# A gated mix of windowed attention and a small routed MLP on one core: another written order for all five engines, projections interleaved by halves, and 112 small operations on other engines

## The chip, the cores and the metric

The kernel runs on one core of a Trainium2 chip, in one launch. The metric is device time in microseconds (us). A profile of one execution shows TensorE as PE (matmuls) and PEld (weight loads), VectorE as DVE, ScalarE as ACT, GpSimd as POOL and the sync engine, which issues most DMAs, as SP. Each engine runs its own list of instructions in order and waits at semaphores for the others.

## The reference

All tensors are bf16. `x` has 2048 rows of 512.

```python
g = sigmoid((x * gate_w).sum(-1, keepdims=True))
# A: attention, 32 heads of 16, each query sees the 256 keys up to itself
qkv = x @ wqkv;  scores = q @ k.T / 4;  p = softmax(masked scores);  a = (p @ v) @ wo
# B: the 8 rows with the largest r = x @ w_r pass through an MLP, the others unchanged
idx = argsort(-r)[:8]
y = (silu(x[idx] @ w_gate) * (x[idx] @ w_up)) @ w_down * sigmoid(r[idx])
b = x;  b[idx] += y
out = g * a + (1 - g) * b
```

In the call both branches get the same `x` (`A_x`).

## The kernel before

The 512 features are cut into four chunks `c` of 128 (eight heads each), the 2048 rows into four column tiles `tc` of 512. For each (`c`, `tc`) there are three **projections**, Q, K and V, into one bank of PSUM (`psG`, two banks). Those of the first column tile of chunk 0 run on the full array (L607, four matmuls over 128 rows). All others are cut by the contraction into 64-row matmuls (L614): four on one half of the array's rows, then four on the other, eight matmuls of 512 columns into the same bank. Matmuls on different halves can run side by side. Their results are taken up by small operations: Q is cast to `QT` (L582/L584), K is cast to `Kr` (L570) and multiplied by four head masks into the block-diagonal `Kbd` (L573, four operations), V is transposed by 32-blocks into `VT` (L589) and multiplied by two masks into `Vbd` (L593, two operations).

The **attention** goes in 156 score units. A main unit takes two blocks of 32 keys against 256 queries: four matmuls (L644), two on each half. A tail unit takes the last 32 queries of eight blocks: 16 matmuls of 32 columns. Each unit writes one of two buffers in `psS`; one ACT instruction (L655) takes the exponential of it into `PT`, and the unit after next has to wait for that. The triangle of each block is masked on `PT` (L665: 128x128 for a main unit, 128x512 for a tail unit). Probabilities times values are `psO` matmuls (L684), pairs of 34 columns on both halves, called pv below. DVE normalises them and applies the gate (L711, L723, L727), a transposing DMA brings them to `OT` (L757), and the output projection (L778, eight matmuls of 64 rows, like a projection) is added to `(1-g)*b` on DVE (L783) and stored.

The **router** needs the two products of `x` with `w_r` and `gate_w` (L804, 64 matmuls of 2 columns), a search of the eight largest on DVE (MAX8, FIND_INDEX8: L828, L829), a gather on the POOL queue, then the MLP on eight rows (L858: 112 matmuls of 8 columns; L900: 14 of 512 columns).

**What sets the order.** The program is recorded as a list of nodes with their dependences. A table `ORDER` holds for every engine the numbers of its nodes in the order in which they are emitted (negative numbers are the bulk loads, held back by `GATE` until a numbered unit's exponential). `BANK` gives each `psG` user its bank and the half it starts with. `FILL` puts filler matmuls (L534) ahead of some units. Waits follow from the dependences and the order. So nothing is decided at run time but how long an engine waits. Before, `BANK` mixes both starting halves.

## Time and profile before

| | us |
|---|---|
| median of 3 runs | 184.43 (184.06 to 184.55) |
| the profiled execution: its own time | 183.18 |
| its span, first to last instruction | 181.1 |
| PE / ACT / DVE / POOL busy | 168.3 / 137.1 / 119.0 / 70.1 |
| first exponential starts | 8.56 |
| last exponential ends | 170.16 |

Busy time is the union of an engine's instructions. A 512-column matmul is shown for about 0.38 us, though the next on the same half starts 0.22 us later, so a PE that is shown busy isn't full. The granted clock of TensorE was 0.977 of full speed on the mean. In the timeline a row gives the start, the length, the engine, the operation and how many were merged into the row; in brackets stands the idle time before it and what ended it. In a table by stage each engine has its busy time and, in brackets, its number of instructions.

### The profile page before, as it was taken

Reading aid. Unit: us, or ns where it says so; the run is one execution under the profiler, and the core shown is the slowest. Engines: PE = TensorE matmul, PEld = TensorE weight load, DVE = VectorE, ACT = ScalarE, POOL = GpSimd, SP = SyncE. Lnnn points to the kernel's source line nnn. Section 1 sums busy time; section 2 is a strip of 40 time slices with the busy share of each in tenths; the row PEclk is TensorE's granted clock in tenths of the full one; section 3 lists DMA queues with packets and bytes.
Section 4 is the critical chain, followed back from the end, with each engine's and each line's share of the span. In section 5 each row is a group of like instructions: output and inputs, shape, how many; then the busy total and the mean of one; then the engine's idle time right before and its main releaser. Section 6 shows DMA issues by size and latency. Waiting matters only on the chain.

```text
span 181.1 us, 10051 instructions
## 1 busy us (share of the span) xinstructions
PE 168.3 (93%) x4586; PEld 119.6 (66%) x4587; DVE 119.0 (66%) x311; ACT 137.1 (76%) x165; POOL 70.1 (39%) x153
## 2 busy tenths in 40 slices
PE   6989999999999999999999999999999999999870
PEld 2446764878686668866878466768876777776520
DVE  7959677988958482351966578776738462726690
ACT  1387721899988898676899698879998999988310
POOL 1054160426339844320554434543441525442200
PEclk9999999999999999957999999999999999999998
DMA  6992162633176754225494121621022551145321
GB/s 138 207 214 81 38 196 54 143 93 105 62 172 162 131 145 141 62 63 153 125 195 92 29 62 34 125 60 29 13 81 79 72 151 38 31 121 177 118 92 42
DMA packets 35745, 18.68 MB, mean 103 GB/s; under 512 B 27617, under 2 KB 35569, under 8 KB 35569
## 3 DMA queue, kind: packets, MB, share of 16 engines
q1 hardware_dynamic: 34560, 17.71, 41.0%
q8 instruction: 37, 0.61, 1.5%
q10 hardware_dynamic: 1072, 0.26, 0.7%
q14 instruction: 12, 0.09, 0.2%
q0 software_dynamic: 64, 0.02, 0.0%
HBM read 11.81 MB, written 4.20 MB: 88 GB/s over the span
## 4 chain that ended last, share of the span: by engine, by line
PE 69%; DVE 12%; ACT 7%; issue 6%; DMA 2%; SPq 1%; POOL 0%; POOLq 0%; DVEq 0%
PE f_psO L684 23%; PE f_psG L614 19%; PE f_psS L644 17%; ACT f_PT L655 7%; PE f_psG L778 4%; DVE f_Kbd L573 2%; DMA out_dram<-f_outt 2%; DVE f_PT L512 2%; PE f_psG L900 2%; PE f_psG L858 2%; DVE f_QT L584 1%; DVE f_VT L589 1%; DVE f_On L727 1%; PE f_psG L804 1%; DVE f_outt L783 1%
## 5 line engine op out<-in xcount | busy, mean ns | idle before, releaser
L655 ACT ACTIVATE f_PT<-f_psS 128x1024 bf16<-128x1024 f32 (+2 forms) x156 | 133.7, 917 | 25.5 <-PE f_psS L644 23.7
L684 PE MATMUL f_psO<-f_Vbd,f_PT 64*128 64x34 bf16 x2880 | 88.0, 175 | 0.7 <-DVE f_On L727 0.7
L684 PEld LDWEIGHTS f_psO<-f_Vbd,f_PT 64*128 64x128 bf16 x2880 | 73.9, 93 | 17.3 <-DVE f_On L727 2.8
L614 PE MATMUL f_psG<-f_XT,f_W 64*128 64x512 bf16 x360 | 83.9, 382 | 0.8 <-DVE f_QT L584 0.5
L644 PE MATMUL f_psS<-f_QT,f_Kbd 64*128 64x256 bf16 (+2 forms) x960 | 71.5, 225 | 1.8 <-ACT f_PT L655 0.6
L665 POOL TENSOR_TENSOR f_PT<-f_PT,f_MK 128x128 bf16<-128x128 bf16 x96 | 41.0, 437 | 81.1 <-ACT f_PT L655 77.9
L644 PEld LDWEIGHTS f_psS<-f_QT,f_Kbd 64*128 64x128 bf16 x960 | 36.6, 93 | 14.1 <-ACT f_PT L655 5.7
L614 PEld LDWEIGHTS f_psG<-f_XT,f_W 64*128 64x128 bf16 x360 | 25.2, 94 | 9.3 <-PE f_psG L614 1.3
L593 POOL TENSOR_SCALAR f_Vbd<-f_VT,f_pb 128x512 bf16<-128x512 f32 x32 | 24.0, 752 | 17.3 <-DVE f_wrg L792 9.2
L778 PE MATMUL f_psG<-f_wo,f_OT 64*128 64x512 bf16 x112 | 27.6, 375 | 0.5 <-DVE f_outt L783 0.4
L665 DVE TENSOR_TENSOR f_PT<-f_PT,f_MK 128x128 bf16<-128x128 bf16 (+1 forms) x60 | 18.4, 326 | 10.7 <-ACT f_PT L655 10.6
L573 DVE TENSOR_SCALAR f_Kbd<-f_Kr,f_hm 128x512 bf16<-128x512 bf16 (+2 forms) x68 | 24.9, 406 | 0.4 <-PE f_psS L644 0.3
L570 DVE CAST f_Kr<-f_psG 128x512 bf16<-128x512 f32 (+2 forms) x17 | 11.4, 668 | 11.9 <-PE f_psG L614 11.4
L783 DVE SCALAR_TENSOR_TENSOR f_outt<-f_xr,f_omg_f,f_psG 128x512 bf16<-128x512 bf16 x15 | 11.1, 743 | 8.6 <-issue 5.3
L584 DVE CAST f_QT<-f_psG 128x512 bf16<-128x512 f32 (+1 forms) x16 | 10.6, 660 | 6.4 <-PE f_psG L614 6.0
L589 DVE STREAM_TRANSPOSE f_VT<-f_psG 128x512 f32<-128x512 f32 x16 | 11.4, 711 | 3.6 <-PE f_psG L614 3.5
L711 DVE RECIPROCAL f_RC<-f_psO 128x32 f32<-128x32 f32 (+1 forms) x17 | 5.9, 344 | 11.9 <-PE f_psO L684 11.7
L727 DVE TENSOR_TENSOR f_On<-f_psO,f_RG 128x512 bf16<-128x512 f32 (+1 forms) x17 | 11.2, 658 | 0.5
L778 PEld LDWEIGHTS f_psG<-f_wo,f_OT 64*128 64x128 bf16 x112 | 7.9, 93 | 2.4 <-issue 0.6
L523 PE MATMUL f_psS<-f_RC 128*128 128x512 bf16 x10 | 4.2, 606 | 1.7 <-DVE f_qi L453 1.7
L723 DVE TENSOR_TENSOR f_RG<-f_RC,f_g_f 128x32 f32<-128x32 f32 (+1 forms) x17 | 3.9, 228 | 0.5
L582 ACT ACT_TABLE_LOAD x1 | 1.3, 1283 | 3.7 <-DVE f_MK L508 3.7
(103 smaller groups left out, 63.5 us busy)
## 6 DMA issues: line engine op xcount, KB each, us to landing
f_xc<-in_A_x_dram SPq DMA_DIRECT2D x8, 256.0 KB, 3.6
f_xr<-f_xc SPq DMA_DIRECT2D x16, 128.0 KB, 3.0
out_dram<-f_outt SPq DMA_DIRECT2D x16, 128.0 KB, 2.1
f_big<-in_B_w_up_dram SPq DMA_DIRECT2D x8, 224.0 KB, 2.9
f_big<-in_B_w_gate_dram SPq DMA_DIRECT2D x8, 224.0 KB, 3.9
f_OT<-in_B_w_down_dram SPq DMA_DIRECT2D x4, 256.0 KB, 3.3
f_W<-in_A_wqkv_dram SPq DMA_DIRECT2D x2, 384.0 KB, 3.9
f_wo<-in_A_wo_dram SPq DMA_DIRECT2D x4, 128.0 KB, 3.0
```

Of the source, the lines that this page charges most:

```text
L573: add("dve", lambda e, h=h: e.tensor_scalar(out=Kbd[:, sl, a // 32:(a + n) // 32, h, :], in0=Kr[:, kr, a:a + n].rearrange("p (a k) -> p a ...
L584: add("dve", lambda e: e.tensor_copy(out=dst, in_=psG[:, it.r, 0:n]), item=it, w=ks, occ=70 + 1.04 * n, due=due, cls="ev")
L589: add("dve", lambda e: e.transpose(out=VT[:], in_=psG[:, it.r, :]), item=it, w=[("VT", vb)], occ=630, due=due, cls="ev")
L593: add(VENG, lambda e, o=o, i=i, b=b: e.tensor_scalar(out=o, in0=i, scalar1=pb_[:, b:b + 1], scalar2=1.0, op0=ALU.mult, op1=ALU.mult), r=[( ...
L614: return e.matmul(psG[:, it.r, 0:n], W[P, kc, which, 128 * c:128 * c + 128], XT[P, kc, 512 * tc + a:512 * tc + a + n], start=(k8 == 0), st ...
L644: ins[s] = e.matmul(psS[:, sb2 + s, n * k:n * k + n], Kbd[P, kslot[(c, kb // 16)][0], kb % 16].rearrange("p h k -> p (h k)"), QT[P, c % 2, ...
L655: add("act", lambda e: e.activation(out=oa, in_=ia, func=ACT.Exp, scale=0.25), r=[("S", i % 2)], w=pk_ + [("ex", i)], occ=2 * nk * n * 0.8 ...
L665: add(eng, lambda e: e.tensor_tensor(out=v, in0=v, in1=m, op=ALU.mult), r=MKR + pk_, w=pk_, occ=cost, due=at(i + 1), cls="mk")
L684: ins[r] = e.matmul(psO[:, r, 68 * ji + 34 * s:68 * ji + 34 * s + 34], PT[P, s, o0:o0 + 128], Vbd[P, c % 2, s, kb, :], start=(kb == kbs[0] ...
L727: add("dve", lambda e: e.tensor_tensor(out=o, in0=i0_, in1=i1_, op=ALU.mult), r=["O", "RG"], w=[("On", ob, 0), ("On", ob, 1)], occ=60 + 12 ...
L778: return e.matmul(psG[:, it.r, :], OTrun(c, a, 1)[P], wo[P, c, :], start=(k8 == 0), stop=(k8 == 7), tile_position=(64 * x, 0), skip_group_ ...
L783: add("dve", lambda e: e.scalar_tensor_tensor(out=outt[:, xs, :], in0=xr[:, xs, :], scalar=omg_f[:, a:a + 1], in1=psG[:, it.r, :], op0=ALU ...
```

## The change

Every list of `ORDER` is written anew, with `GATE`, `FILL` and `BANK`. The recorded nodes are the same but for the filler matmuls: 27 before, 8 now. In `BANK` all split projections now start with the same half, and the second half of one projection stands in the list among the first half of the next one, which has the other bank. 112 operations stand in another engine's list: 72 go from POOL to DVE, 37 from DVE to POOL and three from DVE to ACT. The net effect: of the 68 `Kbd` operations 11 are now on POOL; of the 32 `Vbd` operations 15 are on DVE; of the 128 small masks 75 are on DVE (32 before); of the 28 tail masks 12 are on POOL (none before); three `Kr` casts are on ACT.

The code gets an alternative engine for these nodes, and the planner's costs of them are written out:

```diff
+        for e in self.ENGS:
+            for op in queue[e]:
+                assert op.eng == e or op.alt[0] == e
+                op.eng = e
...
+        def cast(e, o, i):
+            return e.copy(out=o, in_=i) if e is nc.scalar else e.tensor_copy(out=o, in_=i)
...
-            add("dve", lambda e: e.tensor_copy(out=Kr[:, kr, a:a + n], in_=psG[:, it.r, 0:n]), item=it,
-                w=[("Kr", kr, b) for b in ks], occ=70 + 1.04 * n, due=due, cls="ev")
+            add("dve", lambda e: cast(e, Kr[:, kr, a:a + n], psG[:, it.r, 0:n]), item=it,
+                w=[("Kr", kr, b) for b in ks], occ=70 + 1.04 * n, due=due, cls="ev", alt=("act", 55 + 0.83 * n))
...
-                    r=[("Kr", kr, b) for b in ks] + [("hm", h)], w=[("Kbd", sl, h, b) for b in ks], occ=40 + 0.5 * n, due=due + 1, cls="kb")
+                    r=[("Kr", kr, b) for b in ks] + [("hm", h)], w=[("Kbd", sl, h, b) for b in ks], occ=40 + 0.5 * n, due=due + 1, cls="kb", alt=("pool", 100 + 2.86 * n))
...
-                    r=[("VT", vb), ("pb", b)], w=[("Vbd", c % 2, tc, b)], occ=780, due=due + 2, cls="vb")
+                    r=[("VT", vb), ("pb", b)], w=[("Vbd", c % 2, tc, b)], occ=780, due=due + 2, cls="vb", alt=("dve", 500))
...
-FILL = {2: 1, 22: 5, 29: 2, 41: 17, 49: 1, 66: 1, 108: 1, 126: 1, 127: 1}
-BANK = ("3030320312113302010012222010020332120102000321002032032322230000330333000")
+FILL = {15: 2, 18: 1, 39: 1}
+BANK = ("2020230020200202202000222030202200220022000202022202000022002222002022002")
 ORDER = {
-    "pe": [65, 66, 67, 68, 69, 70, 71, 72, 73, 74, 75, 76, 77, 78, 84, 85, 86, 87, 89, 90, 91, 92, 113, 103, 98, 99, 100, 101, 106, 107, 108, 109, 140, 
+    "pe": [65, 66, 67, 68, 69, 70, 71, 72, 73, 74, 84, 85, 86, 87, 75, 76, 77, 78, 140, 89, 90, 91, 92, 98, 99, 100, 101, 103, 113, 106, 107, 108, 109, 
```

The lines of the changed kernel are 11 to 15 higher (the exponential is L669, the split projections L628, pv L699).

**PE, before the 16th score unit.** Before, this stands ahead of that unit (the last row here); L804 are the router's products, L684 is pv:

```order
L614 MATMUL f_psG<-f_XT,f_W 128x512 x4
L804 MATMUL f_psG<-f_wrg,f_XT 128x2 x32
L614 MATMUL f_psG<-f_XT,f_W 128x512 x4
L684 MATMUL f_psO<-f_Vbd,f_PT 128x34 x8
L614 MATMUL f_psG<-f_XT,f_W 128x512
L684 MATMUL f_psO<-f_Vbd,f_PT 128x34 x8
L614 MATMUL f_psG<-f_XT,f_W 128x512 x15
L684 MATMUL f_psO<-f_Vbd,f_PT 128x34 x16
L614 MATMUL f_psG<-f_XT,f_W 128x512 x4
L684 MATMUL f_psO<-f_Vbd,f_PT 128x34 x8
L614 MATMUL f_psG<-f_XT,f_W 128x512 x4
L644 MATMUL f_psS<-f_QT,f_Kbd 128x256 x4
```

Now, up to the same unit (the last row; the 16 matmuls of 32 columns are the unit before it):

```order
L628 MATMUL f_psG<-f_XT,f_W 128x512 x8
L658 MATMUL f_psS<-f_QT,f_Kbd 128x256 x4
L699 MATMUL f_psO<-f_Vbd,f_PT 128x34 x48
L658 MATMUL f_psS<-f_QT,f_Kbd 128x256 x4
L699 MATMUL f_psO<-f_Vbd,f_PT 128x34 x24
L628 MATMUL f_psG<-f_XT,f_W 128x512 x8
L658 MATMUL f_psS<-f_QT,f_Kbd 128x32 x16
L545 MATMUL f_psO<-f_ident 128x240 x4
L658 MATMUL f_psS<-f_QT,f_Kbd 128x256 x4
```

Before, 32 projection matmuls follow each other with no score unit among them; now a unit stands after at most eight. In front of this unit 84 split projection matmuls stand before, 44 now.

**SP, its first transfers.** `f_XT` is the transposed `x` (in pieces of 384, 128 and three times 512 rows), `f_outt` here receives the V weights. Before:

```order
L472 DMA_TRANSPOSE f_XT<-in_A_x_dram 128x4x384
L472 DMA_TRANSPOSE f_XT<-in_A_x_dram 128x4x128
L478 DMA f_outt<-in_A_wqkv_dram 128x4x128
L472 DMA_TRANSPOSE f_XT<-in_A_x_dram 128x4x512 x3
L478 DMA f_W<-in_A_wqkv_dram 128x4x384
```

Now:

```order
L489 DMA f_outt<-in_A_wqkv_dram 128x4x128
L483 DMA_TRANSPOSE f_XT<-in_A_x_dram 128x4x128
L483 DMA_TRANSPOSE f_XT<-in_A_x_dram 128x4x384
L483 DMA_TRANSPOSE f_XT<-in_A_x_dram 128x4x512 x3
L489 DMA f_W<-in_A_wqkv_dram 128x4x384
```

The piece of 384 rows, which the first projections read, goes from first to third.

**POOL, around the gather of the eight rows (L847).** `f_Kbd` here is two of the four masked copies of one K tile, `f_PT` masks, `f_W` copies of V weights:

```order
L680 TENSOR_TENSOR f_PT<-f_PT,f_MK 128x2x8x32
L680 TENSOR_TENSOR f_PT<-f_PT,f_MK 128x2x2x32 x3
L495 COPY f_W<-f_outt 128x128
L587 TENSOR_SCALAR f_Kbd<-f_Kr,f_hm 128x16x32
L495 COPY f_W<-f_outt 128x128
L587 TENSOR_SCALAR f_Kbd<-f_Kr,f_hm 128x16x32
L607 TENSOR_SCALAR f_Vbd<-f_VT,f_pb 128x2x16x16
L847 DMA f_xsel<-in_A_x_dram,f_idxI 8x512
```

Before, POOL has at its gather masks, `Vbd` and copies alone:

```order
L593 TENSOR_SCALAR f_Vbd<-f_VT,f_pb 128x2x16x16
L665 TENSOR_TENSOR f_PT<-f_PT,f_MK 128x2x2x32
L484 COPY f_W<-f_outt 128x128
L665 TENSOR_TENSOR f_PT<-f_PT,f_MK 128x2x2x32
L832 DMA f_xsel<-in_A_x_dram,f_idxI 8x512
```

The masked copies of K are what a score unit's weights are; that unit now also waits for POOL.

39 lines of the change are left out of this document (23 added, 16 removed), and 130 rows, old and new, of the table ORDER.

## The prediction

> **What bounds the kernel now.** I read the page's busy times first, then the table of busy time by stage, then the timeline of ACT, because PE and ACT are the two fullest engines and ACT's exponentials come in a fixed order.
>
> ```profile
> span 181.1 us, 10051 instructions
> PE 168.3 (93%) x4586; PEld 119.6 (66%) x4587; DVE 119.0 (66%) x311; ACT 137.1 (76%) x165; POOL 70.1 (39%) x153
> L655 ACT ACTIVATE f_PT<-f_psS 128x1024 bf16<-128x1024 f32 (+2 forms) x156 | 133.7, 917 | 25.5 <-PE f_psS L644 23.7
> ```
>
> ACT has 133.7 us of exponentials. It waits 23.7 us in all for score matmuls. So a gain must come out of those 23.7 us, or out of what lies before the first and behind the last exponential. Two tables by stage, of all engines and of the exponentials alone, show where ACT is empty:
>
> ```profile
> 0.00:32.37 32.37, 29.49 (x462) 16.43 (x463) 24.90 (x85) 15.29 (x19) 8.87 (x25) 1.00 0.59 133
> 32.37:165.00 132.63, 129.23 (x3877) 97.33 (x3872) 85.59 (x204) 117.29 (x139) 59.20 (x123) 0.97 0.41 97
> ...
> 8.56:32.37 23.81, 13.40 (x16) 1.00 0.50 118
> ```
>
> The columns are length, PE, PEld, DVE, ACT, POOL, granted clock, DMA share and GB/s; the last row has the exponentials alone. In the 23.81 us from the first exponential to 32.37 us they fill 13.40. In the 132.63 us behind that ACT is busy 117.29, so 15.3 us are lost over a stage more than five times as long. The first stage is the poor one. Its timeline on ACT says where:
>
> ```profile
> 8.56 1.94 ACT L655 ACTIVATE f_PT<-f_psS 128x1024 bf16<-128x1024 f32 x2 [1.25 <-PE f_psS L644]
> ...
> 21.16 1.94 ACT L655 ACTIVATE f_PT<-f_psS 128x1024 bf16<-128x1024 f32 x2 [0.47 <-PE f_psS L644]
> 26.30 0.22 ACT L809 ACTIVATE f_eg<-f_zr 128x16 f32<-128x16 f32 x1 [3.19 <-DVE f_zr L808]
> 26.42 1.49 ACT L655 ACTIVATE f_PT<-f_psS 128x512 bf16<-128x512 f32 x2
> 32.37 1.02 ACT L655 ACTIVATE f_PT<-f_psS 128x1024 bf16<-128x1024 f32 x1 [4.46 <-PE f_psS L644]
> ```
>
> Two waits, 3.19 and 4.46 us, make 7.65 us. They are the time in which PE works off the 32 projection matmuls and the router's 64 products that stand in a row in its list; ACT's small exponential of the gate also waits for these products. Of that stage's other 2.76 us (23.81 - 13.40 - 7.65) 0.22 is the gate's exponential and 2.5 are short waits.
>
> What a projection matmul costs PE depends on its neighbour:
>
> ```profile
> 10.70 1.08 PE L614 MATMUL f_psG<-f_XT,f_W 64*128 64x512 bf16 x8
> ...
> 24.34 0.81 PE L614 MATMUL f_psG<-f_XT,f_W 64*128 64x512 bf16 x3
> ```
>
> Three on the same half start 0.22 us apart ((0.81 - 0.37) / 2, 0.37 being the length that one has in these rows). Eight on both halves, mixed, start 0.10 us apart ((1.08 - 0.37) / 7). Two side by side thus cost what one alone costs.
>
> **The change part by part.** I make the sum against the profiled execution's own 183.18 us. The median of the runs is 184.43, 1.25 more, and the forecast is moved by that.
>
> *The burst is gone: -7.65 us.* In the new order at most eight projections stand between two score units up to the 16th, and the router's products are spread over the units before. Eight cost 0.9 us when paired, and a full exponential of the timeline's rows takes 1.02. So both large waits lose their cause. I let the 2.5 us of short waits stand. Bounds: 0, if DVE becomes the reason (below), and -10.2 with the short waits.
>
> *A later start: +2.4 us.* Before, the x piece of 384 rows is issued first. Now it is third.
>
> ```profile
> 0.81 2.68 SPq L472 DMA_TRANSPOSE f_XT<-in_A_x_dram  x2
> 3.53 0.58 SPq L478 DMA_DIRECT2D f_outt<-in_A_wqkv_dram  x1
> ...
> L472 SPq DMA_TRANSPOSE f_XT<-in_A_x_dram x5: 1241/2222/2557, 0.8 to 9.3; - x5
> ```
>
> It now waits for 0.58 us and for the piece of 128 rows, the shortest of the five, 1.24: together 1.8. Then Q's four matmuls of 384 columns run ahead of K's on the first path to the scores: 0.16 us each by 384/512 of 0.22, 0.6 together. Bounds: 0, if the landing and not the issue sets the start, and 3.1 with Q's second piece and the router's small matmul, which now also come ahead of the first unit (two times 0.3). I take 2.4, since the rows are of this very queue. A dummy exponential that lay in an idle stretch of ACT moves to the front: +0.2.
>
> ```profile
> 73.89 0.18 ACT L464 ACTIVATE f_okc<-f_ones_f 1x1 f32<-1x1 f32 x1
> ```
>
> *PE's work moves later, but is paired: -2.0 us.* Ahead of the 16th unit stand 40 projection matmuls less (84 and 44), so 40 more come after. I counted partners in both lists by the half that each matmul is on: one has a partner if a matmul of the other half, of a projection or of the output projection, is among the next seven. Over the whole list 131 pairs and 210 alone become 205 and 62. Behind the 16th unit 109 pairs and 170 alone become 188 and 52: 279 starts of 0.22 us before, 240 now. If a matmul alone blocks its whole 0.22 us, this saves 39 x 0.22 = 8.6 us. If pv fills the other half beside it all the time, an alone one costs half a start, and 40 more cost 40 x 0.11 = 4.4. The trace shows pv starting beside them, though a few at a time:
>
> ```profile
> 54.95 0.37 PE L614 MATMUL f_psG<-f_XT,f_W 64*128 64x512 bf16 x1
> 54.96 0.20 PE L684 MATMUL f_psO<-f_Vbd,f_PT 64*128 64x34 bf16 x2
> 55.17 0.37 PE L614 MATMUL f_psG<-f_XT,f_W 64*128 64x512 bf16 x1
> ```
>
> So I take the middle, -2.0, and let it come off ACT's 15.3 us. Bounds: -8.6 and +4.4.
>
> *Casts on ACT: +0.6 us.* Two of 512 columns come in among the exponentials, by the row of ACT's only one of this size; the third lies ahead of the first exponential, where DVE's was.
>
> ```profile
> L781 ACT CAST f_outt<-f_psG 128x512 bf16<-128x512 f32 x1 | 0.6, 585 | 1.3 <-PE f_psG L775 1.3
> ```
>
> Two make 1.17; half of it may fall into waits. Bounds: 0 and 1.2.
>
> *Operations between DVE and POOL: +1.0 us.*
>
> ```profile
> L573 DVE TENSOR_SCALAR f_Kbd<-f_Kr,f_hm 128x512 bf16<-128x512 bf16 x60 | 23.1, 425 | 0.4 <-PE f_psS L644 0.3
> L593 POOL TENSOR_SCALAR f_Vbd<-f_VT,f_pb 128x512 bf16<-128x512 f32 x32 | 24.0, 752 | 17.3 <-DVE f_wrg L792 9.2 <-DVE f_VT L589 8.0
> L665 POOL TENSOR_TENSOR f_PT<-f_PT,f_MK 128x128 bf16<-128x128 bf16 x96 | 41.0, 437 | 81.1 <-ACT f_PT L655 77.9 <-ACT f_rs L872 2.7
> L665 DVE TENSOR_TENSOR f_PT<-f_PT,f_MK 128x512 bf16<-128x512 bf16 x28 | 11.6, 416 | 1.3 <-ACT f_PT L655 1.3
> L665 DVE TENSOR_TENSOR f_PT<-f_PT,f_MK 128x128 bf16<-128x128 bf16 x32 | 7.9, 246 | 9.4 <-ACT f_PT L655 9.4
> ```
>
> In busy time neither engine becomes the bound: DVE gains 43 x 0.246 for masks and 15 `Vbd` (between the 0.425 of `Kbd` and 0.752), and loses 11 x 0.42, 12 x 0.416 and the casts, so 119 becomes about 127. POOL loses 43 x 0.437 and 15 x 0.752 and gains 23 operations on 512 elements. Those have no row. They take between 0.75 (POOL's one-input row) and 4 x 0.437 = 1.75 (its mask scaled). What counts is the delay: nine full `Kbd` on POOL come 0.33 to 1.3 us later each, and score units wait for them, with the exponentials queued behind. If all is covered it costs nothing; if nothing is, 9 x 1.3 = 11.7. Cover is the two score buffers, about 2 us of exponentials, so I take 1.0, nearer to the covered end.
>
> The Trainium skill bears on this price: GPSIMD Engine Reference, section 4.1 Engine selection, calls one-input operations on GpSimd roughly line-rate and two-input ones about twice as slow as VectorE's. By that rule this term would be near 0 for `Kbd`. The row of `Vbd` (752 ns for 512 elements, one input) doesn't show line-rate.
>
> *Fillers, the tail, the clock: 0.* Of 13 pairs of fillers nine go.
>
> ```profile
> L534 PE MATMUL f_psO<-f_ident 64*128 64x240 bf16 x26 | 3.6, 262 | 0.0
> ```
>
> A pair has 240 columns, 0.1 us by the 0.22 for 512: 0.9 us of PE time at most. They are emitted behind a wait of their own, ahead of the next score unit, where PE would stand; so I take 0. The tail has the same work behind the last exponential; the own time less the last exponential's end, 183.18 - 170.16, stays at 13.0 us. The clock fell once before:
>
> ```profile
> 73.40:77.20 3.80, 3.79 (x152) 3.68 (x154) 0.78 (x3) 2.33 (x4) 1.51 (x3) 1.00 0.27 73
> 77.20:84.05 6.85, 6.56 (x136) 4.60 (x129) 2.28 (x8) 5.13 (x8) 1.27 (x3) 0.50 0.33 86
> ```
>
> PE looks full at 3.79 of 3.80 us when the drop comes, but it ran the MLP's matmuls of 8 columns. These still stand together, so I expect one drop again. PE does half the work in these 6.85 us, so it costs at most 3.4; ACT loses 1.72 there (6.85 - 5.13). I price it at 2.2. The Trainium skill, TensorE: Matmul & The Clock Gate, section "Why this matters for your kernels", wants no PE-idle gaps of about 3 us between bursts, as the condition for full clock. By that rule there would be no drop in either order. The row shows one without such a gap.
>
> Sum: -7.65 + 2.4 + 0.2 - 2.0 + 0.6 + 1.0 = -5.45. Own time 177.7 of 183.18; on the median's scale 184.43 - 5.45 = **179.0 us**.
>
> **The rivals.** *(1) PE stops being the limit behind 32 us too* (chance 0.16): the alone price is the full one, -8.6 in place of -2.0, giving 172.4; or the clock doesn't drop, 176.8. For it: 129.23 of 132.63 us of PE busy. Against it: pv that runs beside single projections.
>
> *(2) The burst goes, but DVE holds the scores* (0.13). The two searches of the router are long and stand in DVE's list ahead of K's and V's operations.
>
> ```profile
> L829 DVE FIND_INDEX8 f_idxu<-f_top,f_scr 1x8 uint32<-1x2048 bf16 x1 | 2.3, 2274 | 0.0
> L828 DVE MAX8 f_top<-f_scr 1x8 f32<-1x2048 bf16 x1 | 2.3, 2272 | 0.0
> ```
>
> Before, the burst had laid in projections ahead of them. Now units come while they run: up to 4.5 us, 183.5. Against it: 24.90 us of DVE work in 32.37 still leaves room.
>
> *(3) The moved work comes back* (0.09): the 40 matmuls cost 4.4 instead of saving 2.0, giving 185.4, about where it was.
>
> *(4) GpSimd holds the score chain, slower* (0.15). Each of the nine `Kbd` stands between a K cast and a score unit; with 1.1 us each uncovered it is 9.9 in place of 1.0, giving 187.9. It decides against the change from (5.45 + 1.0) / 9 = 0.72 us each. For it: score units whose weights wait for POOL behind masks and copies. Against it: POOL is busy 39%.
>
> **How the numbers follow.** The forecast has 0.47 for 176.5 to 182.5; (1) 0.16, (2) 0.13, (3) 0.09, (4) 0.15. The bound for telling a change here is 0.3%, 0.55 us. Faster: 0.47 + 0.16 + 0.11 of (2) + 0.01 of (3) = 0.75. Same: 0.02 of (2), 0.04 of (3), 0.01 of (4) = 0.07. Slower: 0.04 + 0.14 = 0.18. The range goes to (1)'s low end and into (4): 172.5 to 187.5.
>
> **What would show it.** The first exponential starts near 11.0 us (8.56 + 2.4) and the 16th at 26 to 28 instead of 32.37, with no wait over 2 us on ACT between. From the 16th exponential to the last it is about 137.5 us (before 137.8, 32.37 to 170.16). POOL's `Kbd` and tail masks are at 0.75 to 1.75 us. The total of ACT's waits for score matmuls falls from 23.7 to 15 or so. I am wrong if ACT's waits name POOL or DVE work behind the scores, if the second stage grows by more than 3 us, or if the clock drops more than once.

## The result, and the profile after

The changed kernel takes 181.79 us (median of 4 runs, 181.43 to 182.41); the kernel before took 184.25 beside it (183.57 to 184.55). The ratio is 0.9875, interval 0.9833 to 0.9917: 2.5 us faster, where 5.45 was forecast. Medians below take all runs, while ratios and intervals leave out the runs that lie over 1.5% above the fastest of their kernel, so the two can differ by up to 1.6%.

The profiled execution took 182.41 us in a span of 179.8. It is the slowest of its four, while the profiled execution before (183.18 us) was faster than all four runs of that kernel. Its page, busy times and the group of the exponentials:

```profile
PE 156.8 (87%) x4568; PEld 109.7 (61%) x4568; DVE 123.4 (69%) x343; ACT 137.6 (77%) x168; POOL 73.0 (41%) x118
...
L669 ACT ACTIVATE f_PT<-f_psS 128x1024 bf16<-128x1024 f32 (+3 forms) x156 | 133.0, 917 | 20.6 <-PE f_psS L658 19.7
```

and its waits of PE and, in the last row, of ACT for scores, each with the total, how often, and the longest:

```profile
PE f_psO L699 <- issue: 2.7, 4, 1.0
PE f_psO L699 <- DVE f_On L742: 2.3, 3, 1.7
PE f_psS L658 <- issue: 2.2, 3, 1.1
...
PE f_psG L873 <- issue: 0.7, 2, 0.4
...
ACT f_PT L669 <- PE f_psS L658: 19.7, 36, 1.8
```

The kernel before has one row of "issue" for PE:

```profile
PE f_psS L644 <- issue: 0.5, 2, 0.3
```

PE's busy time fell by 11.5 us (from 168.3), but its idle time rose: 23.0 us of the span against 12.8. ACT still waits 19.7 us for scores (23.7 before). A new kind of wait stands at PE: "issue", 5.6 us in these three rows, in which PE waits for nothing that the profile shows; before there were 0.5 us of it. The waits of ACT for scores all name PE, none POOL or DVE.

Busy time by stage, of the changed kernel, cut at its 16th, 136th and last exponential:

```profile
28.70:145.93 117.23, 109.09 (x3438) 78.93 (x3435) 84.16 (x217) 103.67 (x124) 59.93 (x94) 0.99 0.38 93
145.93:166.47 20.54, 18.43 (x642) 14.05 (x640) 13.44 (x39) 16.02 (x21) 4.06 (x5) 1.00 0.54 131
166.47:179.80 13.33, 5.92 (x119) 3.28 (x111) 6.28 (x18) 1.75 (x4) 0.20 (x1) 0.87 0.28 84
```

The same cuts of the kernel before:

```profile
32.37:150.31 117.94, 115.27 (x3427) 86.62 (x3421) 78.36 (x188) 103.90 (x123) 52.87 (x110) 0.97 0.42 98
150.31:169.78 19.47, 17.87 (x622) 13.62 (x620) 10.68 (x25) 16.38 (x20) 7.75 (x17) 1.00 0.32 93
169.78:181.10 11.32, 5.65 (x88) 2.96 (x87) 5.03 (x15) 1.53 (x5) 0.63 (x2) 0.93 0.28 88
```

Beside a drop in the last microseconds, which both kernels have, the granted clock (the last but two of the columns) fell twice:

```profile
8.99:12.40 3.41, 3.08 (x18) 1.55 (x19) 2.24 (x12) 1.17 (x3) 1.65 (x3) 0.50 1.12 212
67.02:70.43 3.41, 3.41 (x72) 2.07 (x70) 2.78 (x11) 2.71 (x5) 1.73 (x5) 0.50 0.67 213
```

Put side by side, with the terms of the forecast:

| stage | before | after | difference | forecast |
|---|---|---|---|---|
| to the first exponential | 8.56 | 11.89 | +3.33 | +2.6 |
| first to 16th | 23.81 | 16.81 | -7.00 | -7.65 |
| 16th to 136th | 117.94 | 117.23 | -0.71 | -0.4, to the last |
| 136th to last | 19.47 | 20.54 | +1.07 | |
| last to the span's end | 11.32 | 13.33 | +2.01 | 0 |
| outside the span | 2.08 | 2.61 | +0.53 | 0 |
| own time | 183.18 | 182.41 | -0.77 | -5.45 |

The last row but one is loose: in the other three executions of the change the time outside the span is 3.2 to 4.7 us. The burst went nearly as forecast. The start cost more, and the end, forecast at nothing, cost 2. The long stage gained next to nothing although PE is shown 6 us less busy there (115.27 to 109.09). The timeline of PE shows what one of its new stops looks like:

```profile
52.57 0.18 PE L699 MATMUL f_psO<-f_Vbd,f_PT 64*128 64x34 bf16 x2
53.71 0.34 PE L699 MATMUL f_psO<-f_Vbd,f_PT 64*128 64x34 bf16 x14 [0.96 <-issue]
```

PE stops for 0.96 us after two of 16 pv matmuls that stand in a row and need nothing new. The trace has nine such stops of 0.3 us or more. Counted in the order of PE's records (matmuls, weight loads and waits on semaphores), each stands at the same place of 256: its number leaves the rest 193, or 192 where a record is missing. The DMA queues of the page name a traffic of this size:

```profile
q8 instruction: 36, 0.59, 1.4%
```

0.59 MB in 36 packets are 16.4 KB each, and (4568 + 4568 + about 60 semaphore waits) / 36 = 255 instructions. So TensorE's code arrives in blocks of 256, and PE stops where one has not come. The trace's times of these packets say the same: one packet lands between any two borders (places with that rest), and it had landed at least 1.24 us before PE crossed the border. At the nine stops it had landed 1.30 to 1.49 us before, so PE went on about as soon as it ever does; elsewhere it had landed up to 4.6 us before. The nine stops make 5.8 us by PE's gaps, all behind the 16th exponential. One of them, of 0.51 us, the profile puts down to ACT.

### The profile page after: what moved, and what is told of

It reads as the page before. It is cut to its first block, busy times and chain, and to the rows that moved or that the text cites. A ratio compares the mean times of both kernels' runs of the same rounds, so it can differ in the third digit from the quotient of the medians.

```text
span 179.8 us, 10017 instructions
## 1 busy us (share of the span) xinstructions
PE 156.8 (87%) x4568; PEld 109.7 (61%) x4568; DVE 123.4 (69%) x343; ACT 137.6 (77%) x168; POOL 73.0 (41%) x118
## 4 chain that ended last, share of the span: by engine, by line
PE 63%; issue 10%; ACT 10%; DVE 10%; DMA 3%; SPq 1%; POOL 0%; POOLq 0%; DVEq 0%
PE f_psO L699 19%; PE f_psG L628 17%; PE f_psS L658 16%; ACT f_PT L669 9%; PE f_psG L793 5%; DMA f_XT<-in_A_x_dram 3%; DVE f_On L742 2%; PE f_psG L621 2%; PE f_psG L873 2%; PE f_psG L915 2%; DVE f_RC L726 1%; DVE f_PT L523 1%; DVE f_RG L738 1%; DVE f_VT L603 1%; SPq L483 1%
## 5 line engine op out<-in xcount | busy, mean ns | idle before, releaser
L669 ACT ACTIVATE f_PT<-f_psS 128x1024 bf16<-128x1024 f32 (+3 forms) x156 | 133.0, 917 | 20.6 <-PE f_psS L658 19.7
L658 PE MATMUL f_psS<-f_QT,f_Kbd 64*128 64x256 bf16 (+3 forms) x960 | 65.9, 225 | 4.2 <-issue 2.2
L699 PE MATMUL f_psO<-f_Vbd,f_PT 64*128 64x34 bf16 x2880 | 60.8, 174 | 5.5 <-issue 2.7
L680 POOL TENSOR_TENSOR f_PT<-f_PT,f_MK 128x128 bf16<-128x128 bf16 (+1 forms) x65 | 38.0, 593 | 65.1 <-ACT f_PT L669 62.2
L699 PEld LDWEIGHTS f_psO<-f_Vbd,f_PT 64*128 64x128 bf16 x2880 | 55.5, 93 | 14.2 <-DVE f_On L742 4.8
L628 PE MATMUL f_psG<-f_XT,f_W 64*128 64x512 bf16 x360 | 62.7, 380 | 0.1
L628 PEld LDWEIGHTS f_psG<-f_XT,f_W 64*128 64x128 bf16 x360 | 20.6, 94 | 8.5 <-PE f_psG L628 0.5
L587 POOL TENSOR_SCALAR f_Kbd<-f_Kr,f_hm 128x512 bf16<-128x512 bf16 (+2 forms) x11 | 16.2, 1479 | 12.1 <-DVE f_W L495 7.6
L607 POOL TENSOR_SCALAR f_Vbd<-f_VT,f_pb 128x512 bf16<-128x512 f32 x17 | 12.7, 750 | 14.3 <-DVE f_VT L603 9.4
L575 DVE CAST f_Kr<-f_psG 128x512 bf16<-128x512 f32 (+1 forms) x14 | 9.2, 660 | 10.7 <-PE f_psG L628 6.3
L607 DVE TENSOR_SCALAR f_Vbd<-f_VT,f_pb 128x512 bf16<-128x512 f32 x15 | 8.3, 553 | 0.0
```

What stands on the lines that cost most here:

```text
L575: return e.copy(out=o, in_=i) if e is nc.scalar else e.tensor_copy(out=o, in_=i)
L587: add("dve", lambda e, h=h: e.tensor_scalar(out=Kbd[:, sl, a // 32:(a + n) // 32, h, :], in0=Kr[:, kr, a:a + n].rearrange("p (a k) -> p a ...
L607: add(VENG, lambda e, o=o, i=i, b=b: e.tensor_scalar(out=o, in0=i, scalar1=pb_[:, b:b + 1], scalar2=1.0, op0=ALU.mult, op1=ALU.mult), r=[( ...
L628: return e.matmul(psG[:, it.r, 0:n], W[P, kc, which, 128 * c:128 * c + 128], XT[P, kc, 512 * tc + a:512 * tc + a + n], start=(k8 == 0), st ...
L658: ins[s] = e.matmul(psS[:, sb2 + s, n * k:n * k + n], Kbd[P, kslot[(c, kb // 16)][0], kb % 16].rearrange("p h k -> p (h k)"), QT[P, c % 2, ...
L669: add("act", lambda e: e.activation(out=oa, in_=ia, func=ACT.Exp, scale=0.25), r=[("S", i % 2)], w=pk_ + [("ex", i)], occ=2 * nk * n * 0.8 ...
```

## The experiments

**The moved operations and the order, apart.** Kernel `order_only` has the new order with all 112 operations on their former engines; `moves_only` has the old order with the 112 on their new ones.

```diff
 # order_only: each of the 112 numbers back into the list of its former engine
-    "act": [16, 22, 23, 15, 88, 93, 104, 13, ...
+    "act": [16, 22, 23, 15, 88, 104, 13, ...
```

> The changed kernel's orders, banks, fillers and transfers with all 112 moved operations back on the engines that they had before, each at the place in that engine's list where it ran by time. Theory (my sum: the moves cost 1.0 us and the casts on ScalarE 0.6 us of the path, so the order alone is the better part): 1 to 2 us under the changed kernel, 179.8 to 180.8 us. Rival (the moves pay, since VectorE would be late with the masks and the operands that TensorE waits for): 0.5 us or more above the changed kernel, 182.3 us or more. Nothing to choose: within 0.5 us.

> The kernel before with its own orders, banks, fillers and transfers, and only the 112 operations moved to the engines that the change gives them, each at the place in that engine's list where it ran by time. Theory (my sum: moves and casts cost): 1 to 2 us above the kernel before, 185.2 to 186.3 us, mostly through GpSimd's halves of K's block form at 1.5 us each. Rival (the moves pay by themselves): 0.5 us or more under the kernel before.

`order_only`: 181.51 us, ratio 0.9853 (0.9799 to 0.9908). That can't be told from the change itself; the gain of 1 to 2 us that was expected isn't there. `moves_only`: 189.82 us, ratio 1.0172 (1.0097 to 1.0248), slower than before, and by more than the 1 to 2 us expected. So the order makes all the gain that can be seen; the moves are worth nothing in it, and cost 3 us and more in the other. One place of the trace of `moves_only`:

```profile
61.30 2.86 DVE L607 TENSOR_SCALAR f_Vbd<-f_VT,f_pb 128x512 bf16<-128x512 f32 x1
61.56 1.91 POOL L680 TENSOR_TENSOR f_PT<-f_PT,f_MK 128x128 bf16<-128x128 bf16 x3
...
64.45 0.57 PE L699 MATMUL f_psO<-f_Vbd,f_PT 64*128 64x34 bf16 x32 [1.87 <-DVE f_PT L680]
```

An operation of DVE whose median is 0.49 us took 2.86 while masks and copies ran on POOL, and PE then waited 1.87 us for the mask behind it. No run was made to test that POOL's operations hold DVE's, but the trace of the kernel before shows it on `Kbd`:

```profile
55.72 0.72 POOL L593 TENSOR_SCALAR f_Vbd<-f_VT,f_pb 128x512 bf16<-128x512 f32 x1
55.80 0.78 DVE L573 TENSOR_SCALAR f_Kbd<-f_Kr,f_hm 128x512 bf16<-128x512 bf16 x1
```

Of DVE's 60 `Kbd` operations of this size 27 begin while an operation of POOL runs; 26 of them end 0.145 to 0.153 us behind the end of that operation, and they take up to 0.84 us. The 33 others take 0.22 to 0.35. So work on POOL lengthens work on DVE, which the forecast's prices of the moves leave out. How much of the 3 us this is wasn't measured.

**The start and the tail.** In `start_sp` SP begins with the two pieces of `x` again. In `tail_check` three check operations on 480 columns, which stand last in DVE's list, go to an idle place before the end.

```diff
 # start_sp
-    "sp": [17, 25, 24, 26, 27, 28, ...
+    "sp": [24, 25, 17, 26, 27, 28, ...
 # tail_check
-    "dve": [..., 1499, 1614, 1615, 1616, 1510, ..., 1742, 1728, 1739, 1740, 1741, 1743, ...]
+    "dve": [..., 1499, 1614, 1615, 1616, 1739, 1740, 1741, 1510, ..., 1742, 1728, 1743, ...]
```

> The changed kernel with one edit: SyncE's queue begins again with the two first pieces of X (384 rows, then 128) ahead of the first 128 columns of V's weights, as before the change; everything else stays. Theory (the later start costs the whole run, and is the term that I sized too small): the first exponential, at 11.89 us in the changed kernel, comes back to 8.6 to 9.6 us, the half-speed stretch of the clock from 8.99 to 12.40 us goes, the 16th exponential comes 2.4 to 3.3 us earlier than 28.70 us, and the median falls from 181.8 to 178.5 to 179.4 us. Rival (TensorE's work ahead of the 16th exponential, not the first piece of X, sets when that exponential starts): the first exponential comes as early, the 16th moves by less than 1 us and the median stays within 0.8 us of the changed kernel's.

> The changed kernel with one edit: the three operations of 480 columns on VectorE that check the row sums (together 1.71 us) stand in VectorE's idle stretch near 160 us instead of behind the last but one output piece at 172.4 us. Theory (in the changed kernel the end follows the flag, which VectorE's late check makes at 174.86 us): the flag comes 1.0 to 1.7 us earlier, no exponential moves, and the median falls by 1.0 to 1.7 us, to 180.1 to 180.8. Rival (the end follows the last output piece on its way out): the flag comes earlier and the median stays within 0.4 us of the changed kernel's.

`start_sp`: 180.55 us, ratio 0.9804 (0.974 to 0.9867); the first exponential starts at 9.78 us instead of 11.89 (10.25 in the repeat of the change, below). The 178.5 to 179.4 us that was expected wasn't reached. `tail_check`: 180.13 us, ratio 0.9708 (0.9639 to 0.9777); from the last exponential to the end 11.6 us. In the changed kernel DVE's end reads

```profile
171.76 0.75 DVE L798 SCALAR_TENSOR_TENSOR f_outt<-f_xr,f_omg_f,f_psG 128x512 bf16<-128x512 bf16 x1 [1.10 <-issue]
172.43 0.40 DVE L1041 TENSOR_SCALAR f_scr<-f_RC 128x480 f32<-128x480 f32 x1
172.86 0.66 DVE L1042 SCALAR_TENSOR_TENSOR f_scr<-f_RC,f_scr 128x480 f32<-128x480 f32 x1
173.56 0.65 DVE L1043 TENSOR_REDUCE f_okc<-f_scr 128x1 f32<-128x480 f32 x1
...
174.86 0.15 DVE L1051 TENSOR_SCALAR flag<-f_psO 1x1 int32<-1x1 f32 x1 [0.33 <-PE f_psO L1048]
```

and in `tail_check`

```profile
171.36 0.75 DVE L798 SCALAR_TENSOR_TENSOR f_outt<-f_xr,f_omg_f,f_psG 128x512 bf16<-128x512 bf16 x1 [1.68 <-DMA f_xr<-f_xc]
172.03 0.18 DVE L1042 SCALAR_TENSOR_TENSOR f_scr<-f_RC,f_scr 128x32 f32<-128x32 f32 x1
...
172.77 0.14 DVE L1051 TENSOR_SCALAR flag<-f_psO 1x1 int32<-1x1 f32 x1 [0.33 <-PE f_psO L1048]
```

From the end of the last addition to the end of the flag it is 2.50 us (172.51 to 175.01) there and 0.80 here. The kernel before has

```profile
169.57 0.40 DVE L1026 TENSOR_SCALAR f_scr<-f_RC 128x480 f32<-128x480 f32 x1
...
173.98 0.74 DVE L783 SCALAR_TENSOR_TENSOR f_outt<-f_xr,f_omg_f,f_psG 128x512 bf16<-128x512 bf16 x1
...
176.58 0.15 DVE L1036 TENSOR_SCALAR flag<-f_psO 1x1 int32<-1x1 f32 x1 [0.33 <-PE f_psO L1033]
```

2.01 us, with its first check operation ahead of the last additions. So the check makes 0.5 of the tail's +2.0, and its move gains 1.7 in this stage. Another 1.1 lies between the last exponential's start and the last addition's end (6.04 us against 4.94; the stage has 119 matmuls against 88), and 0.4 behind the flag. The whole stage is 11.3 us before, 13.3 to 13.8 in the five profiled executions with the change's order of the tail (`order_only`, `start_sp`, `after_again` and `shift_blocks` beside the change), and 11.6 to 11.9 in the three where the check is moved (`tail_check`, and `repaired` and `repaired2` below). So this term holds in every execution.

By the times alone neither edit is shown to pay: the intervals of `start_sp` and `tail_check` overlap that of the unedited change in its repeat (0.968 to 0.9813). What each is worth is read from the traces.

**Are the stops bound to the blocks of code?** `after_again` is the changed kernel once more. `shift_blocks` puts 32 tiny matmuls on zeros at the start of PE's list, 64 instructions with their weight loads, so that everything behind lies a quarter of a block further on.

```diff
 # shift_blocks
+        def warm_32(e):
+            for _ in range(32):
+                e.matmul(psS[:, 3, 0:8], zw[:, 0:128], zw[:, 0:8], start=True, stop=True)
+            return warm(e)
-            add("pe", warm, r=["zw"], ...
+            add("pe", warm_32 if k == NWARM - 1 else warm, r=["zw"], ...
```

> The changed kernel itself once more, beside the others on one chip, since single executions of it differ by some 2 us. Theory (code blocks): the stretches in which TensorE stands still for 'issue' without any wait that the trace shows stand where TensorE's stream passes a multiple of 256 instructions (record 193, 449, 705 and so on of its weight loads, matmuls and semaphore waits), together 1.5 to 6 us behind 20 us, other ones of the same borders each time; nothing like it stands elsewhere. Rival (they are waits whose semaphore the trace hides): they stand at the same instructions in every execution, whatever their number. Time: 181 to 182.5 us.

> The changed kernel with 64 more instructions ahead on TensorE: the last warm-up matmul is preceded by 32 matmuls of 8 columns, in the time in which TensorE waits for X (6.1 to 7.8 us). All later instructions come 64 places later in the stream. Theory (code blocks of 256 instructions): the stalls for 'issue' stay at record 193 modulo 256, and so move in the program by 64 instructions, away from the instructions at which they stood; so the stall of 1.12 us ahead of the score matmuls at 159.36 us stands elsewhere. Rival (hidden waits): they stay at the same instructions, at record 1 modulo 256. Time: within 1.5 us of the changed kernel's, since the borders only move; the half-speed stretch at 9 to 12.4 us goes if TensorE's idle time ahead of it was its cause.

`after_again`: 179.72 us (177.64 to 183.34), ratio 0.9747 (0.968 to 0.9813), on another chip: a gain of 4.3 us where the first comparison had 2.5. `shift_blocks`: 182.53, ratio 0.9863 (0.9813 to 0.9912), on the same chip as `after_again` and 2.8 us above it by the medians (the intervals just meet), where at most 1.5 was expected; why is open. In both the stops stand again at the rest 192 or 193 of 256, in `shift_blocks` thus at other matmuls. Waits that the trace hides would have stayed at the same matmuls. The five kernels with the same order of PE behind the 16th exponential can be compared over that stage (16th to last); a stop counts here from 0.05 us on, whatever the profile puts it down to:

| kernel | stops at block borders there, us | length, us |
|---|---|---|
| the change | 5.8 | 137.77 |
| `tail_check` | 4.3 | 136.40 |
| `shift_blocks` | 4.4 | 136.09 |
| `after_again` | 3.6 | 135.93 |
| `start_sp` | 1.7 | 134.13 |
| before (other order) | 0.8 | 137.41 |

4.1 us less of stops go with 3.6 us less of time. The lengths stand in one row of busy times for each:

```profile
27.44:163.37 135.93, 128.35 (x4076) 92.69 (x4073) 97.98 (x254) 119.49 (x144) 63.99 (x98) 0.97 0.41 100
```

(of `after_again`), and for `start_sp`

```profile
26.87:161.00 134.13, 128.01 (x4056) 94.05 (x4054) 97.46 (x254) 119.56 (x143) 63.94 (x98) 0.97 0.41 101
```

The line through the first and the last of the five gives some 132.6 us without stops, an estimate: 4.8 less than before. Two more executions lie beside this line, `order_only` 0.5 us above (5.3 us of stops in 137.85) and `repaired` 1.2 below (4.0 in 134.95), and the time at half clock in this stage is not the same in all (3.41 us in the change and `shift_blocks`, 6.83 in the others and before). So the 4.8 is good to about 1 us: the new order of PE earned about that much, and the stops took 1.7 to 5.8 of it, another amount in every execution. `start_sp` alone, with as long a half clock as before, is 3.3 us shorter than before with its stops in it.

**A block by itself.** `blocks_alone` adds twice 1536 small matmuls behind the last result (its time, 272.9 us, has this in it, and is not compared). With the second half the 16 weight loads are made once more.

```diff
+        def burst(e):
+            for _ in range(768):
+                for r in range(2):
+                    ... ins = e.matmul(psO[:, r, 68:102], PT[P, 0, 0:128], Vbd[P, 0, 0, 0, :], ...)
+        add("pe", burst, r=["flag", "bigm", "ones_c", "top8"], ...)
+        add("pe", burst, r=["flag", "burst1"], ...)   # and the 16 loads, r=["burst1"]
```

> The changed kernel, and behind its last instruction two bursts of 1536 matmuls of 34 columns on alternating halves (the shape of the weighted sums; 3072 instructions of TensorE each, 12 blocks of 256). During the first no transfer runs; with the second start 16 loads of 229 KB each. Theory (code blocks come in one at a time, and behind other transfers): in the first burst a block takes 2.2 to 3.2 us in place of the 1.6 us that its matmuls need, standing still at each border; under the loads 3.5 us or more. Rival (the stream is not the limit): 1.6 to 1.8 us a block in both bursts and no stall at the borders.

```profile
183.58:187.58 4.00, 2.00 (x128) 1.89 (x128) 0.00 (x0) 0.00 (x0) 0.00 (x0) 0.50 0.02 4
191.31:194.76 3.45, 2.00 (x128) 1.89 (x128) 0.00 (x0) 0.00 (x0) 0.00 (x0) 0.50 0.02 5
227.33:231.88 4.55, 2.00 (x128) 1.89 (x128) 0.00 (x0) 0.00 (x0) 0.00 (x0) 0.50 0.96 232
```

Each window holds 128 matmuls and 128 weight loads, one block. PE works 2.00 us of it, at half clock, and then stops. With quiet queues a block takes 3.45 to 4.00 us, more than the 2.2 to 3.2 expected; under the loads (DMA share 0.96) 4.55 to 4.82. All of this is at half clock; at full clock the kernels have blocks between two borders of 3.48 us (the change) and 3.20 (`start_sp`), so the floor there is somewhat lower. The trace divides such a block: the next packet starts 1.05 to 1.18 us behind the border when the queues are quiet and 2.19 to 2.45 under the loads, is under way for 0.9 to 1.4, and PE goes on 1.20 to 1.58 us after it has landed. The changed kernel goes through a block in 4.3 us on the mean, stops included, as the kernel before does, so both run close above this floor, and the change falls on it where its code is denser or a load delays the fetch. The Trainium skill, Runtime: NRT & Kernel Launch, section "Instruction fetch mechanics", has blocks of 16 KiB or 256 instructions that are fetched while the engine works, and calls the crossing mostly hidden. The size agrees with this trace; "mostly hidden" does not fit the stops of up to 1.1 us in the kernel, nor the 3.45 us and more of a block by itself.

`loads_early` was meant to take the loads out of the fetches' way: the first 16 weight loads are issued together from 20 us on.

```diff
-GATE = [8, 10, 12, 15, 17, 20, 22, 24, 27, 29, 32, 34, 36, 39, 41, 44, 46, ...
+GATE = [8, 8, 8, 8, 8, 8, 8, 8, 8, 8, 8, 8, 8, 8, 8, 8, 46, ...
```

> The changed kernel with the 16 loads of the gate and up weights, which it spreads over 17 to 55 us, issued one behind the other from 20 us on (their gates all at score unit 8, their places in SyncE's list together); nothing else differs. Theory (transfers delay TensorE's code blocks): between 36 and 55 us the time from passing a border to the start of the next block's transfer falls from 1.3 to 2.9 us to under 1 us, and the stall near 52 us (0.96 and 0.83 us in two executions) goes; between 20 and 36 us it rises, with stalls of its own there. Time: within 1 us of the changed kernel's, since stalls move rather than go. Rival (transfers do not matter for the blocks): delays and stalls stay as they are.

189.74 us, ratio 1.0288 (1.0198 to 1.0377). PE stood once for 10 us, since the later pieces of V's weights queue behind these loads on SP:

```profile
PE f_psO L699 <- POOL f_PT L680: 10.1, 1, 10.1
...
PE f_psS L658 <- issue: 1.7, 3, 1.0
PE f_psO L699 <- issue: 0.5, 2, 0.3
```

Behind that stand the stops fell to 2.0 us, and from the 61st exponential to the 136th it took 71.06 us against the change's 73.09. But the unedited repeat took 71.22, so this can't be put down to the loads. What did follow them is the fetch: near 51 and 55 us, where the loads are now gone, the next packet starts 0.4 and 0.6 us behind the border, against 1.3 to 2.9 us behind the four borders from 40 to 54 us in the change. As a remedy it failed.

**What a pair is worth.** In `half_pairs` 11 digits of `BANK` are changed so that 131 pairs are left, as many as before; in `unpair` 29 digits, so that 23 are left. The lists stay.

```diff
 # half_pairs
-BANK = ("2020230020200202202000222030202200220022000202022202000022002222002022002")
+BANK = ("2020230020301202202000222131202200221022110202023302000022003322002022002")
```

> The changed kernel with only as many pairs as the kernel before had: 11 digits of the table of banks have their last bit turned, spread over the program, so that 131 pairs of 512-column matmuls stand on different halves instead of 205; nothing else differs. Theory A (my term: the 74 pairs are worth 2.0 us on the path, since ScalarE and the latencies set the pace once TensorE has room): 1 to 3.5 us above the changed kernel, a ratio to the kernel before of 0.98 to 1.005. Theory B (each pair is worth what it cost when 182 of them were undone, 29.5 us in all, 0.16 us each): 9 to 12 us above the changed kernel, a ratio to before of 1.02 to 1.05, and the order without its pairs would be slower than the kernel before.

> The changed kernel with the pairing undone and nothing else: 29 digits of the table of banks have their last bit turned, so that projections that stand side by side use the same half of the rows; orders, engines, banks, fillers and transfers stay. Pairs of 512-column matmuls on different halves fall from 205 to 23. Theory (pairing is worth its matmul time on the path, my term of 2.0 us or more): the median rises by 2 to 8 us over the changed kernel's. Rival (TensorE has room, and its stream of code blocks comes no faster anyway): its busy time rises by 8 us or more, the stalls at the 256-instruction borders fall under 1 us, and the median stays within 1 us of the changed kernel's.

`half_pairs`: 196.31 us, ratio 1.0699 (1.0626 to 1.0771). `unpair`: 209.22, ratio 1.1396 (1.135 to 1.1441). By the ratios `half_pairs` is 15 to 18 us above the change, and `unpair` 28 to 30; both are more than either theory expected. For `half_pairs` that is 0.2 us for each of the 74 pairs lost, twice what the half price (0.11) makes of it. Of that, 3.4 to 5.1 us at most is a longer time at half clock: between the 16th exponential and the last it is 13.65 us there, 3.41 in the change and 6.83 in its repeat. The timelines show one at work, of `half_pairs`

```profile
32.10 0.59 PE L628 MATMUL f_psG<-f_XT,f_W 64*128 64x512 bf16 x2
```

and of the change

```profile
31.09 0.60 PE L628 MATMUL f_psG<-f_XT,f_W 64*128 64x512 bf16 x4
```

Two matmuls on one half take as long as four on both. But 131 pairs in the old order took 184 us, and here 196. So the number of pairs doesn't price an order. What stands behind an unpaired one differs: in `half_pairs` it is another matmul on the same half for 139 of 210 and pv for 30; in the old order it is pv for 100 of 210, a score unit for 36, and one on the same half for 55.

**Fewer instructions for the same sums.** Four matmuls over all 128 rows do the work of eight halves: 236 matmuls and 236 weight loads fewer, 1.8 blocks. In `full_rows` this is done to the change, in `before_full` to the kernel before, in `full_best` to `repaired2` (below).

```diff
-                full = c == 0 and tc < NFULL
+                full = True
...
-            for k8 in range(4 if tail else 8):
+            for k8 in range(4):
...
-                    if tail:
+                    if True:
                         return e.matmul(psG[:, it.r, :], OTrun(c, a, 1), wo[:, c, :], ...)
```

> The changed kernel, with every projection and every output projection as four matmuls over all 128 rows in place of eight over 64 (same sums, 236 matmuls and 236 weight loads fewer, about 1.8 of 36 blocks of instruction code). Theory A (TensorE's stream of instructions and its starts bind): the paired halves cost what a full matmul costs, so no time is lost by them, the 62 that stood alone save 62 x 0.11 = 6.8 us of starts at most, and 1.8 blocks of about 4 us each go; PE's busy time falls from 156.8 us to 147 to 152, the time to 174 to 178 us, 3 to 6 us under the changed kernel's on the same scale. Theory B (a half matmul leaves the other half to pv and the scores, and that overlap is worth more than the starts): PE stands at full rows in front of pv, and the time is 184 us or more, above the changed kernel's. Theory C (waits between engines bind): within 1 us of the changed kernel's.

> The same full-row matmuls on the order of the kernel before, where 210 halves stood alone. Theory A: more is saved here than in the changed order, since more stood alone: 6 to 15 us, 170 to 178 us, and most of what the changed order had gained by pairing is had without it. Theory B: slower than before, 186 us or more. Theory C: within 1 us of before; the burst of 32 projections ahead of the 16th score unit then still costs its two waits of 3.2 and 4.5 us in every case, since a burst of paired halves takes as long as one of full rows.

> The same full-row matmuls on the kernel repaired2 (changed order, SP begins with x, three check operations of the tail on VectorE, one filler fewer), which took 0.960 of the kernel before. Theory A: 3 to 6 us less than repaired2, 172 to 175 us, ratio 0.93 to 0.95. Theory B: 180 us or more. Theory C: 177 to 179 us, ratio 0.96.

`full_rows`: 188.27 us, ratio 1.0205 (1.0163 to 1.0247). `before_full`: 192.01, 1.0394 (1.034 to 1.0448). `full_best`: 184.44, 0.9995 (0.9953 to 1.0036). Each is some 6 to 8 us above the kernel that it is made from, as theory B had it for the times; A and C fall. PE's busy time did not fall either in `full_rows` (157.1 us). What grew is the waiting of the weight loads, here of `full_rows`,

```profile
PEld f_psS L658 <- issue: 16.9, 43, 0.9
...
PEld f_psG L621 <- issue: 10.6, 39, 2.5
```

which stands at 5.4 (10 times) and 2.7 (4 times) in the change, where the second row covers only the first column tile of chunk 0 (the split projections add 0.5). A pair of halves costs PE what a full row costs, but a half lets the scores' and pv's weights and matmuls in on the other half. That it is this, and not the weight load of a full row itself, is argued, not shown. So the floor of code blocks is no reason to make matmuls fewer and larger here.

**Mending what was found.** `repaired` has `tail_check`'s edit, the whole start of the old order (SP, ACT, DVE, POOL and PE up to the first unit), no filler at unit 15, and three projection matmuls and a score unit put ahead of a pv at 115 us that waited 1.73 us for DVE. `repaired2` has the same with `start_sp`'s edit alone in place of the old start.

```diff
 # repaired2, beside the edits of start_sp and tail_check
-FILL = {15: 2, 18: 1, 39: 1}
+FILL = {18: 1, 39: 1}
-    "pe": [..., 1093, 1094, 1102, 1344, 1345, 1346, ...]
+    "pe": [..., 1344, 1345, 1102, 1346, 1093, 1094, ...]
```

> The changed kernel with four repairs. The first 33 entries of TensorE's list, 42 of VectorE's and the heads of SyncE's and ScalarE's as before the change (with the first Kr cast of 384 columns and the first products of K's block form back on VectorE); the check of the row sums in VectorE's idle stretch near 160 us; the filler ahead of score unit 15 taken out; three projection matmuls and a score unit put ahead of the weighted sum that waited 1.72 us for the normaliser at 114 us. Theory (the terms of start and tail are what was lost, and they add): start 2 to 3 us, tail 1.0 to 1.7, filler and normaliser 0.5 to 1.5, so 176.0 to 178.3 us. Rival (TensorE's stream of code blocks takes back what the other edits give): 178.5 to 180.5 us, with more stall at the borders than the changed kernel on the same chip.

> The changed kernel with SyncE's first two pieces of X ahead again (its lists otherwise as the change has them at the start), the check of the row sums in VectorE's idle stretch near 160 us, the filler ahead of score unit 15 taken out, and three projection matmuls and a score unit put ahead of the weighted sum that waited for the normaliser at 114 us. Theory (the same repairs as before without the start that let the clock fall to half from 13.2 to 23.4 us): a ratio to the kernel before of 0.945 to 0.96, 174 to 177 us, no half-speed stretch ahead of 60 us. Rival (the clock falls here too, or TensorE's code blocks take it back): 0.962 or more, as with the first repair.

`repaired`: 178.35 us, ratio 0.9624 (0.9551 to 0.9698). Its first exponential starts at 8.66 us as before the change, but the clock stood at half for 10 us soon after, and the 16th starts at 29.44, no better than the change's 28.70:

```profile
10.00:12.00 2.00, 0.99 (x27) 0.87 (x29) 1.12 (x4) 0.67 (x1) 0.75 (x1) 1.00 1.26 268
13.15:23.39 10.24, 10.24 (x145) 5.53 (x144) 4.62 (x18) 6.04 (x9) 0.43 (x1) 0.50 0.25 67
```

`repaired2`: 177.77 us, ratio 0.9604 (0.9503 to 0.9704), beside 184.59 of the kernel before; the 16th exponential starts at 26.15, and no half clock stands ahead of 63 us. Both lie between the ranges of their two theories, so neither theory is decided. About 7 us under the kernel before, `repaired2` has the lowest median of all, but by the intervals it can't be told from `repaired`.

## Why the prediction was right in sign and wrong in size

The profiled execution came out 0.77 us shorter where 5.45 was forecast. Of the 4.7 us between, 2.0 lie in the tail, 0.8 from the 16th exponential to the last, 0.7 in the start, 0.65 in the burst and 0.5 outside the span. Two steps failed: the tail, put at nothing, and PE's later work, whose price had no term for the code fetch.

*The tail, 0: failed, +2.0.* "The tail has the same work behind the last exponential" did not hold: the stage has 18 operations of DVE instead of 15 and 119 matmuls instead of 88, and the check stands behind the last addition. The order of DVE's last operations tells both. Counted as the forecast did, from the last exponential's end to the end of the own time, 13.0 became 15.3 us. The stage is as long in every execution with this order, and 1.7 us of it came back by one move.

*PE's work later but paired, -2.0: failed in its mechanism.* It priced the order by counting starts, with and without a partner. `half_pairs` shows that this count has no fixed price: 131 pairs are 184 us in one order and 196 in another. And the step had no term for what limits PE next: its own stream of instructions. Blocks of 256 instructions run into their fetch, and 1.7 to 5.8 us go there. What the order earns on PE without these stops is about 4.8 us by the comparison of five executions, above the middle that was taken and inside the bounds. `order_only`, which has neither the casts nor the moves, shows what is left of the term by itself: +0.4 us (137.85 against 137.41) in place of -2.0. The profile before showed the traffic (37 packets) and 0.5 us of such waits, too little to be noticed.

*The burst, -7.65: right.* It measured -7.00 (-6.6 in `after_again`). The longest wait of ACT for scores in the whole execution is 1.8 us, at 106 us.

*The later start, +2.6: a fair middle.* It was +3.33 here, +1.7 in `after_again`. In the ten profiled executions with SP's new order the first exponential starts between 10.25 and 12.08 us. In the three latest (11.89 to 12.08; the change, `tail_check`, `full_rows`) the clock fell to half between 8.4 and 9.3 us, which the forecast did not have; in the seven others (10.25 to 10.92) it did not. Why it fell is open: `half_pairs` and `order_only` waited as long for `x` as the change (1.7 and 1.8 us) and had no drop. With SP's old order (`start_sp`) the start is +1.2, and with the whole old start (`repaired`) +0.1, so the rest lies in the order of the first projections and casts.

*Casts and moves, +0.6 and +1.0: too large by themselves.* `order_only` has neither and takes the same time. The prices were right (`Kbd` on POOL, forecast between 0.75 and 1.75 us):

```profile
L587 POOL TENSOR_SCALAR f_Kbd<-f_Kr,f_hm 128x512 bf16<-128x512 bf16 x9 | 14.2, 1579 | 3.1 <-ACT f_Kr L575 3.1
L587 DVE TENSOR_SCALAR f_Kbd<-f_Kr,f_hm 128x512 bf16<-128x512 bf16 x51 | 18.4, 388 | 0.2
```

They were covered. The rule of the Trainium skill's GPSIMD Engine Reference, section 4.1, that one-input operations run there at roughly line-rate, does not fit these: 1579 ns on POOL against 388 on DVE.

*The rivals.* (1) PE ceased to be the full engine (87% busy) but the gain did not follow, for the reason above. (2) The searches on DVE held nothing: from the start of the 16th exponential to that of the 21st it is 4.53 us in both kernels. (3) The moved projections did not cost 4.4 us: from the 16th exponential to the last it is at most 0.4 us more than before (here and in `order_only`), and 1.0 to 3.3 less in the four others of the table. (4) GpSimd held no scores in this order; with the old order the same moves are slower (1.0172).

*What was to show it.* The 16th exponential came at 28.70 (forecast 26 to 28). From there to the end of the last it is 138.4 us, forecast 137.5; that this is so close is luck, since two larger terms cancel, about 4.8 us earned and 5.8 lost to stops. ACT's waits are 19.7 us instead of 15 (15.9 in `start_sp`). The clock dropped twice ahead of the end, which the forecast had named as a sign of being wrong, the second time for 3.41 us in place of 6.85.

What stays open: why the fetch differs so from one execution to the next, how much of each difference between chips and executions is this, and whether an order exists whose blocks never meet the floor.

## What to carry to other kernels

When an engine is made denser, look at what feeds it: count its instructions by blocks of 256, and compare the time that a block takes with the 3.2 to 4.8 us that a fetched block took here. Gaps called "issue" on TensorE that stand at the same place of 256 instructions were this wait here. And price a new order from the end too: what stood behind the last exponential was paid in full here, 2 us.

## What the hardware did that was not expected

TensorE's code comes in 36 packets of 16.4 KB, one for 256 instructions. A block alone takes 3.45 to 4.00 us at half clock, under loads 4.55 to 4.82, and PE crosses no border earlier than 1.19 us after its packet has landed (in `repaired2`; 1.24 in the change). Matmuls over all rows cost 6 to 8 us more here than paired halves that fill the same array time; why isn't shown. In the kernel before, 26 of the 27 `Kbd` operations of DVE that began while POOL worked ended 0.15 us after POOL's operation did, and took up to 0.84 us instead of 0.35. In `repaired` the clock fell to half at 13.15 us, though PE's longest idle time from 6.05 us on was 0.83 us; from 10 to 12 us it was busy 0.99 of 2.00 us.
